# K and V tiles loaded as two halves of 64 partitions from two queues, and w_down in 14 tiles of 128 rows: a decode kernel of two attention and two gated layers

## The chip, the cores and the metric

One core of a Trainium2 chip runs the whole program. The metric is device time in microseconds (us) of one execution. For a program on one core, a run counts as "slow" when it lies over 1.5% above the fastest run of the same kernel, and slow runs are left out of ratios. A ratio below is the mean time of one kernel's fast runs over the mean of the other's fast runs of the same rounds, so it isn't quite the ratio of the medians that are quoted. A kernel is called faster or slower only when its whole interval lies beyond 2%.

In the profile lines PE is TensorE (matmuls), PEld its weight loads, DVE VectorE, ACT ScalarE, POOL GpSimd and SP SyncE. A partition is one of the 128 rows of SBUF, the on-chip memory into which tiles are loaded. A load is cut into packets, which 16 DMA engines move; "DMA share" is the time of all packets over the time of the 16 engines, so 1 means that all are busy. The granted clock (PEclk) is TensorE's clock as a share of full speed.

## The reference, cut to what matters

```python
# B=4 batches, one query row each, D=512; 32 query heads, 8 K/V heads, 4096 positions, head size 128, F=1792; bf16
def A(x, k_cache, v_cache, wq, wo):        # attention over the cache
    q = (x @ wq).reshape(B, 1, 32, 128)...
    p = softmax(q @ k.T * 128**-0.5)       # each K/V head serves 4 query heads
    return (p @ v)... @ wo
def Bm(x, w_gate, w_up, w_down):           # gated block
    return (sigmoid(x @ w_gate) * (x @ w_up)) @ w_down

x = x + A(layernorm(x), k_cache, v_cache, wq, wo)
x = x + Bm(layernorm(x), w_gate, w_up, w_down)
x = x + A(layernorm(x), k_cache, v_cache, wq, wo)     # the same caches and weights again
x = x + Bm(layernorm(x), w_gate, w_up, w_down)
```

K and V of one head and one batch are 1 MB each. Both layers read all of them: 2 x 8 x 4 x 2 tiles of 1 MB, 134 MB of the 148 MB that the kernel loads. The rest are weights, which are loaded once, in the first layer.

## The kernel before

A "group" is one K/V head of one layer (16 groups); each needs four K tiles and four V tiles (one for each batch). All tiles go through a ring of ten buffers, all by SyncE's queue, and a load waits until the tile that had its buffer has been used. Each K tile is transposed in place by VectorE before TensorE multiplies.

```python
    ring = [sb(f"ring{i}", [P, T * DH], bf) for i in range(NS)]     # P=128, T*DH=4096, NS=10
    wd = sb("wd", [FR, 4, 4, D], bf)                                # FR=112: 1792 = 112 * 16
    ...
    def load_kv(n, kind, b):
        s = len(tiles) % NS
        ...
        if kind == "k":      # each partition: one run of 8 KB
            i = A_k[b, g].rearrange("(p t) d -> p (t d)", p=P)
            o = dst[:]
        else:                # each partition: four runs of 2 KB
            i = A_v[b, g].rearrange("(a p t) d -> p a (t d)", a=4, p=P)
            o = dst[:].rearrange("p (a x) -> p a x", a=4)
        S.put("sp", lambda e: e.dma_start(o, i), writes=[f"r{s}"], dma=f"r{s}")
    ...
        (7, "k"): [lambda: load_w(          # w_down goes out after the K tiles of group 7
            "wd", wd[:].rearrange("r j c n -> r j (c n)"), B_wd.rearrange("(j r c) n -> r j (c n)", j=4, c=4)
        )],
```

The only other work of GpSimd is building constants at the start and one small operation (`rstd`) in each of the four norms.

## Time and profile before

| | before |
|---|---|
| time, median of 2 runs | 415.18 us (414.91 to 415.44) |
| bytes read | 148.1 MB, all K, V and weights on one queue |
| rate in layer 2, where nothing but K and V is loaded (260 to 370 us) | 403 GB/s |
| VectorE waiting for K loads, in total (view of waits) | 53 us |
| TensorE waiting for V loads, in total (view of waits) | 12 us |

These are lines of the page of before: the share of time in which the 16 DMA engines were busy (tenths, 40 slices of the span), the rate in each slice; then two groups of instructions (busy us, mean ns of one, then idle time just before them and what ended most of it); then the DMA issues (KB each, median us from issue to landing).

```profile
DMA  7999999999999999999999919999999999999500
GB/s 260 408 382 413 386 389 406 391 415 386 406 391 394 403 407 415 396 416 281 293 411 396 359 25 392 407 401 405 401 407 399 407 399 407 400 407 399 209 2 0
...
L333 DVE STREAM_TRANSPOSE ring<-ring 128x2048 int32<-128x2048 int32 x64 | 146.2, 2299 | 53.7 <-DMA ring<-in_A_k_cache_dram 53.3
...
L413 PE MATMUL O_ps<-ring,pt_sb 128*16 128x512 bf16 x512 | 57.3, 628 | 27.4 <-ACT pt_sb L374 15.9
...
ring<-in_A_k_cache_dram SPq DMA_DIRECT2D x64, 1024.0 KB, 14.2
ring<-in_A_v_cache_dram SPq DMA_DIRECT2D x64, 1024.0 KB, 16.2
...
wd<-in_B_w_down_dram SPq DMA_DIRECT2D x1, 1792.0 KB, 30.9
```

The DMA engines are busy in nearly every slice, at about 400 GB/s, and the computing engines wait for them: the loads bound the kernel. Four places fall short: the first slice; slices 19 and 20 (281 and 293 GB/s); slice 24 (25 GB/s), where all ten buffers are full and the chain of matmuls and norms between the layers has to finish; and the end. The load of w_down takes twice as long to land (30.9 us) as the typical load of K or V (14 to 16 us).

The view of stretches gives the same in numbers. Its columns are: from and to, length, busy us and instructions of each computing engine, granted clock of TensorE, share of DMA time, GB/s.

```profile
core 0: us, PE busy (x) PEld busy (x) DVE busy (x) ACT busy (x) POOL busy (x), PEclk, DMA share, GB/s
187.00:208.00 21.00, 5.93 (x39) 1.64 (x38) 10.30 (x6) 2.41 (x2) 0.00 (x0) 0.50 1.03 288
239.00:249.50 10.50, 5.00 (x72) 2.34 (x72) 3.08 (x7) 1.65 (x6) 0.54 (x1) 0.67 0.14 24
260.00:370.00 110.00, 61.58 (x570) 25.13 (x568) 63.72 (x74) 26.91 (x56) 0.00 (x0) 0.60 1.03 403
```

The DMA view of 186 to 210 us alone, in 40 slices of 0.6 us, shows what happens around the load of w_down:

```profile
DMA  9999999999998999999999999999999999999999
GB/s 410 410 423 437 437 396 410 253 218 253 205 171 191 225 266 253 212 218 218 215 242 198 215 218 201 229 239 239 277 369 375 369 386 376 379 389 393 382 399 382
```

While the packets of w_down are in flight, the rate stays between 171 and 277 GB/s, about 225 in the mean and little over half of the normal one, although the engines are fully busy.

The trace also keeps each DMA packet with its size and time. Worked out from that record (medians):

```
before   K packets     8192 B   313 ns      (8192)
before   V packets     2048 B    88 ns      (34816, with those of wq)
before   w_down        4096 B   294 ns      (448)
```

The 66 K packets that start while those of w_down do (189.8 to 205.5 us) take 547 ns in the mean and 566 in the median.

### The profile page before, as it was taken

What the parts mean: (1) busy time and instruction counts of PE and PEld (TensorE: products, weight loads), DVE (VectorE), ACT (ScalarE), POOL (GpSimd) and SP (SyncE); (2) the same over time, 40 slices, a digit from 0 to 9 for tenths busy, and PEclk for the clock granted to TensorE, in tenths of its full rate; (3) what the DMA queues carried; (4) which work ended last, traced back from release to release, by engine and by line L of the source; (5) the groups of instructions that cost most, each with busy time, mean ns of one, the idle gap of its engine ahead of it and who ended that gap; (6) DMA issues with size and microseconds to landing.
All of it is one profiled execution on the core that took longest, in us unless ns stands there. A gap on an engine that the chain in (4) does not pass through costs nothing.

```text
span 415.9 us, 4348 instructions
## 1 busy us (share of the span) xinstructions
PE 203.4 (49%) x1784; PEld 84.8 (20%) x1784; DVE 205.9 (50%) x259; ACT 82.5 (20%) x179; POOL 6.7 (2%) x24
## 2 busy tenths in 40 slices
PE   0047343473545447352316745475745555654556
PEld 0013111121212212120002222131312222221122
DVE  3823627346272825516316626473829283838221
ACT  1031040210403031040210014132231303030300
POOL 4000000000000000000000000000000000000000
PEclk9985565555555555555555766655556666566659
DMA  7999999999999999999999919999999999999500
GB/s 260 408 382 413 386 389 406 391 415 386 406 391 394 403 407 415 396 416 281 293 411 396 359 25 392 407 401 405 401 407 399 407 399 407 400 407 399 209 2 0
DMA packets 50067, 148.40 MB, mean 357 GB/s; under 512 B 2232, under 2 KB 6336, under 8 KB 41600
## 3 DMA queue, kind: packets, MB, share of 16 engines
q1 hardware_dynamic: 50048, 148.13, 93.6%
q8 instruction: 14, 0.23, 0.2%
q14 instruction: 5, 0.04, 0.0%
HBM read 148.12 MB, written 0.00 MB: 356 GB/s over the span
## 4 chain that ended last, share of the span: by engine, by line
issue 40%; DMA 28%; PE 14%; DVE 7%; SPq 6%; ACT 4%; POOL 0%; POOLq 0%; ACTq 0%; DVEq 0%
DMA ring<-in_A_k_cache_dram 24%; PE S_ps L342 5%; SPq L222 5%; DMA ring<-in_A_v_cache_dram 5%; DVE ring L333 3%; PE O_ps L413 3%; ACT p_sb L358 2%; PE Y_ps L499 2%; PE M_ps L429 1%; DVE ml L352 1%; SPq L235 1%; PE Y_ps L446 1%; PE PT_ps L471 1%; PE O_ps L471 1%; ACT o_sb L424 1%
## 5 line engine op out<-in xcount | busy, mean ns | idle before, releaser
L333 DVE STREAM_TRANSPOSE ring<-ring 128x2048 int32<-128x2048 int32 x64 | 146.2, 2299 | 53.7 <-DMA ring<-in_A_k_cache_dram 53.3
L342 PE MATMUL S_ps<-ring,qbd 128*16 128x512 bf16 x512 | 57.0, 620 | 82.4 <-DVE ring L333 81.4
L358 ACT ACTIVATE p_sb<-S_ps,nbias 128x1024 bf16<-128x1024 f32 x16 | 40.4, 2522 | 185.8 <-DVE nbias L355 185.8
L413 PE MATMUL O_ps<-ring,pt_sb 128*16 128x512 bf16 x512 | 57.3, 628 | 27.4 <-ACT pt_sb L374 15.9
L352 DVE TENSOR_REDUCE ml<-S_ps 128x1 f32<-128x1024 f32 x16 | 19.6, 1224 | 60.9 <-PE S_ps L342 60.9
L342 PEld LDWEIGHTS S_ps<-ring,qbd 128*16 128x16 bf16 x512 | 15.4, 120 | 121.2 <-DVE ring L333 81.5
L429 PE MATMUL M_ps<-sel_o,o_sb 128*128 128x16 f32 x128 | 26.9, 349 | 14.0 <-ACT o_sb L424 14.0
L429 PEld LDWEIGHTS M_ps<-sel_o,o_sb 128*128 128x128 f32 x128 | 25.3, 294 | 28.5 <-ACT o_sb L424 28.5
L317 PE MATMUL Q_ps<-qT,perm 128*128 128x16 bf16 x64 | 4.4, 179 | 51.5 <-ACT qT L314 51.5
L446 PE MATMUL Y_ps<-wo,oT 128*4 128x512 bf16 x64 | 26.5, 560 | 4.7 <-ACT oT L435 4.7
L413 PEld LDWEIGHTS O_ps<-ring,pt_sb 128*16 128x16 bf16 x512 | 15.8, 125 | 56.9 <-issue 38.8
L379 DVE STREAM_TRANSPOSE tr<-ml 128x64 f32<-128x64 f32 x16 | 3.9, 245 | 42.2 <-ACT qT L314 37.0
L424 ACT ACTIVATE o_sb<-O_ps,wcol 128x512 f32<-128x512 f32 x16 | 11.0, 687 | 68.3 <-PE O_ps L413 64.6
L323 ACT ACTIVATE qbd<-Q_ps 32x64 bf16<-32x64 f32 x64 | 13.7, 214 | 6.6 <-PE Q_ps L317 6.0
L317 PEld LDWEIGHTS Q_ps<-qT,perm 128*128 128x128 bf16 x64 | 2.9, 107 | 52.8 <-ACT qT L314 52.8
L369 PE MATMUL PT_ps<-sel_p,p_sb 128*128 128x64 bf16 x128 | 9.4, 238 | 8.3 <-ACT p_sb L358 8.3
L393 DVE TENSOR_TENSOR el<-ee,tr 128x16 f32<-128x16 f32 x16 | 2.8, 175 | 20.2 <-ACT ee L392 20.2
L309 PEld LDWEIGHTS Q_ps<-xnT,wq 128*128 128x128 bf16 x256 | 7.9, 102 | 13.3 <-issue 12.9
L309 PE MATMUL Q_ps<-xnT,wq 128*128 128x4 bf16 x256 | 9.2, 166 | 1.6 <-DMA wq<-in_A_wq_dram 1.3
L374 ACT ACTIVATE pt_sb<-PT_ps 128x512 bf16<-128x512 f32 x16 | 9.6, 597 | 1.9 <-PE PT_ps L369 1.5
L456 DVE SCALAR_TENSOR_TENSOR x_row<-Y_ps,x_row 4x512 f32<-4x512 f32 x4 | 2.7, 679 | 14.0 <-PE Y_ps L446 8.8
L293 PE MATMUL M_ps<-sel_h,xn 4*128 4x4 bf16 x16 | 1.2, 173 | 16.9 <-DVE xn L286 16.9
(53 smaller groups left out, 88.7 us busy)
## 6 DMA issues: line engine op xcount, KB each, us to landing
ring<-in_A_k_cache_dram SPq DMA_DIRECT2D x64, 1024.0 KB, 14.2
ring<-in_A_v_cache_dram SPq DMA_DIRECT2D x64, 1024.0 KB, 16.2
wq<-in_A_wq_dram SPq DMA_DIRECT2D x4, 1024.0 KB, 14.9
wo<-in_A_wo_dram SPq DMA_DIRECT2D x4, 1024.0 KB, 14.8
wg<-in_B_w_gate_dram SPq DMA_DIRECT2D x1, 1792.0 KB, 15.7
wu<-in_B_w_up_dram SPq DMA_DIRECT2D x1, 1792.0 KB, 15.7
wd<-in_B_w_down_dram SPq DMA_DIRECT2D x1, 1792.0 KB, 30.9
x_io<-in_A_x_dram SPq DMA_DIRECT2D x1, 4.0 KB
```

The source lines that it names most:

```text
L222: S.put("sp", lambda e: e.dma_start(o, i), writes=[f"r{s}"], dma=f"r{s}")
L309: fns.append(lambda e, h=h, k=k, c0=c0: e.matmul(Q_ps[:, h * B:(h + 1) * B], lhsT=wq[:, k, c0:c0 + DH], rhs=xnT[:, k, :], start=(k == 0), ...
L323: fns.append(lambda e, a=a: e.activation(qbd[32 * a:32 * a + 32, qi, :, :, a * R:(a + 1) * R], Q_ps[32 * a:32 * a + 32, 64:128].rearrange( ...
L333: S.put("dve", lambda e: e.transpose(v, v), reads=[f"r{s}"], writes=[f"r{s}"])
L342: fns.append(lambda e, q=q, nn=nn, b=b, kt=kt: e.matmul(S_ps[32 * b:32 * b + 16, q * 512:(q + 1) * 512], lhsT=qbd[:, qi, b, nn, :], rhs=kt ...
L352: "dve", lambda e: e.tensor_reduce(ml[:, 0:1], S_ps[:], AX.X, ALU.max, negate=True),
L358: lambda e: e.activation(p_sb[:].rearrange("p tb (j q) -> p q tb j", q=4), S_ps[:].rearrange("p (q tb j) -> p q tb j", q=4, tb=8), ACTF.Ex ...
L374: "act", lambda e: e.activation(pt_sb[:].rearrange("p t x -> p (t x)"), PT_ps[:], ACTF.Copy),
L413: fns.append(lambda e, tb=tb, b=b, v=v: e.matmul(O_ps[32 * b:32 * b + 16, :], lhsT=pt_sb[:, tb, 16 * b:16 * b + 16], rhs=v[:, :, tb, :], s ...
L424: "act", lambda e: e.activation(o_sb[:], O_ps[:], ACTF.Copy, scale=wcol[:, 0:1]),
L429: fns.append(lambda e, a=a: e.matmul(M_ps[:, 0:16], lhsT=o_sb[:, a * P:(a + 1) * P], rhs=sel_o[:, a, :], start=(a == 0), stop=(a == 3),))
L446: fns.append(lambda e, h=h: e.matmul(Y_ps[0:B, :], lhsT=oT[:, g * R + h, :], rhs=wo[:, g * R + h, :], start=(g == 0 and h == 0), stop=(g = ...
```

## The change

The intent: more bandwidth from two queues that work at the same time, and an end to the dip at w_down, whose load has 112 partitions. Each K and V tile is cut into partitions 0 to 63, issued by SyncE, and 64 to 127, issued by GpSimd. w_down is laid out as three chunks of 128 rows for each quarter of F (12 tiles) and two tiles that stack the four remainders of 64 rows.

```diff
-    wd = sb("wd", [FR, 4, 4, D], bf)
+    wd = sb("wd", [P, 4, 3, D], bf)
+    wd_r = sb("wd_r", [P, 2, D], bf)
...
-        S.put("sp", lambda e: e.dma_start(o, i), writes=[f"r{s}"], dma=f"r{s}")
+        for q, eng in ((0, "sp"), (1, "pool")):
+            if kind == "k":
+                oo, ii = o[64 * q:64 * q + 64], i[64 * q:64 * q + 64]
+            else:
+                oo, ii = o[64 * q:64 * q + 64], i[64 * q:64 * q + 64]
+            S.put(eng, lambda e, oo=oo, ii=ii: e.dma_start(oo, ii), writes=[f"r{s}{'ab'[q]}"], dma=f"r{s}{'ab'[q]}")
...
+    def load_wd():
+        rows = B_wd.rearrange("(j f) n -> j f n", j=4)
+        load_w("wd", wd[:]..., rows[:, 0:FM, :].rearrange("j (p c) n -> p j (c n)", c=3))     # FM = 384
+        for i in range(2):
+            load_w(f"wd_r{i}", wd_r[i * FR:(i + 1) * FR], rows[2 * i:2 * i + 2, FM:FS, :]...)  # FR = 64
...   (readers of a tile wait for both halves; the down projection has 14 matmuls instead of 16)
```

## The prediction

> **What bounds the kernel now.** The loads do. The page shows 148.1 MB on one queue, 93.6% of the engines' time; the table of stretches gives 400 GB/s from 10.4 to 187 us and 403 GB/s from 260 to 387 us while PE and DVE are half busy. In the raw packet records a K packet (8 KB) takes 313 ns and a V packet (2 KB) 88 ns: about 12 ns fixed and 27 B/ns per engine, so the limit (estimate: 16 x 27.2 = 435 GB/s) is only 8% away. Losses outside that: the start (260 GB/s for 10 us); 187 to 208 us at 288 GB/s; 239 to 249.5 us, where the ten ring buffers are full and the chain waits for GLU, norm and scores (24 GB/s); and a tail of 28 us after the last loads.
>
> **w_down.** The loss at 187 to 208 us is the load of w_down: 448 packets of 4 KB took 294 ns instead of about 163 (estimate from 12 ns + 27 B/ns), the load landed after 30.9 us, and its neighbours were slowed too (K packets to about 546 ns, V to 119). The DMA view shows a flat 215 GB/s there, half rate. My reading: with 112 partitions engines share SBUF ports. The stretch lost about 21 x (1 - 288/400) = 5.9 us. Loads of 128 partitions plus two small ones of 64 should win back 4 to 6 us. It is on the critical path (values of group 7 wait 8.7 us for V right after). Two matmuls less save under 0.5 us per layer.
>
> **Halves.** Bytes and packet sizes stay; the number of K/V issues doubles. SyncE isn't short of issue time, so a second issuer removes nothing there. What may be gained is the 12 ns between packets, if two rings per engine overlap: at most 7%, mainly V. The risk: each half lies in 64 partitions. The Trainium skill, "SBUF — State Buffer", Door 1, says partitions 0..63 reach eight of 16 ports (196 GB/s measured) and that two concurrent DMAs at partitions 0 and 64 were only 6% faster than one. No run here shows halves, but the 215 GB/s of w_down is the same pattern. With both rings filled, pairs of engines share two ports: taking turns, they keep 400 GB/s; in step, they get about 215. K/V is 134 MB: each 10% of rate lost costs about 35 us.
>
> GpSimd adds about 7 us of constants before its first load (timeline: busy until 7.1 us), during which the lower half runs alone: 1 to 3 us. In layer 1 SyncE's queue also carries 14 MB of weights, so the halves drift apart; a tile is complete only with its slower half.
>
> **Sum.** 415 - 5 (w_down) + 2 (start) = 412 if the halves are neutral; about 395 if overlap pays; 450 to 650 if ports collide. Collision is somewhat likelier than not: predicted 428 us, range 396 to 620. Faster 0.24, same 0.24, slower 0.52.
>
> **What would show it.** Collision: DMA still about 100% busy, GB/s of 260 to 400 in the steady stretches, K packets well over 313 ns, PE and DVE waiting for ring loads. Overlap: 410 to 430 GB/s. w_down: no dip before the layer boundary. Drift: one half's landing time well above the other's.
>
> **What would make it wrong.** Fabric buffering that lets engines take turns by themselves; GpSimd too slow in writing descriptors, so that its half limits; another mapping of 64 partitions to engines.

## The result, and the profile after

The changed kernel takes 622.79 us (621.53 and 624.06), half as much again as before: the ratio is 1.501, with a 95% interval of 1.4918 to 1.5102. The page of the changed kernel, the same lines:

```profile
DMA  8999999999999999999999989999999999999920
GB/s 199 240 270 260 245 233 279 250 241 290 238 228 257 231 256 226 262 273 239 256 238 258 229 193 239 274 240 262 261 245 255 273 250 269 253 265 263 260 43 0
...
q1 hardware_dynamic: 29920, 81.02, 55.9%
q0 software_dynamic: 14336, 67.12, 41.5%
...
L350 DVE STREAM_TRANSPOSE ring<-ring 128x2048 int32<-128x2048 int32 x64 | 147.0, 2306 | 249.7 <-DMA ring<-in_A_k_cache_dram 248.9
L430 PE MATMUL O_ps<-ring,pt_sb 128*16 128x512 bf16 x512 | 56.4, 619 | 161.7 <-DMA ring<-in_A_v_cache_dram 135.2
...
ring<-in_A_k_cache_dram SPq DMA_DIRECT2D x64, 512.0 KB, 26.2
ring<-in_A_v_cache_dram SPq DMA_DIRECT2D x64, 512.0 KB, 29.6
ring<-in_A_k_cache_dram POOLq DMA_DIRECT2D x64, 512.0 KB, 14.9
ring<-in_A_v_cache_dram POOLq DMA_DIRECT2D x64, 512.0 KB, 16.3
```

The DMA engines are as busy as before, to the end, but they move about 250 GB/s instead of 400. The idle time before the K transposes grows from 53.7 to 249.7 us, that of TensorE before the values from 27.4 to 161.7 us; most of both now ends with a load. GpSimd's halves land 15 to 16 us after their issue, SyncE's only after 26 to 30 us.

Two stretches of the changed kernel, the start and a piece of layer 2 (without weight loads):

```profile
0.00:10.40 10.40, 0.00 (x0) 0.00 (x0) 3.34 (x9) 1.28 (x1) 8.00 (x26) 1.00 0.76 188
430.00:580.00 150.00, 50.47 (x468) 21.68 (x468) 52.17 (x66) 24.07 (x55) 19.95 (x35) 0.54 1.03 259
```

Layer 2 runs at 259 GB/s. The packet record shows that the packets themselves became slow (medians):

```
after    K packets, SyncE     8192 B   529 ns      (4096)      before: 313 ns
after    K packets, GpSimd    8192 B   522 ns      (4096)
after    V packets, SyncE     2048 B   142 ns      (18432, with those of wq)   before: 88 ns
after    V packets, GpSimd    4096 B   231 ns      (8192)
```

GpSimd's V packets are twice as large as SyncE's: the same transfer is cut differently by the two queues.

### The profile page after: what moved, and what is told of

Same layout as the page of the kernel before. It is cut to its first block, busy times and chain, and to the rows that moved or that the text cites. A ratio compares the mean times of both kernels' runs of the same rounds, so it can differ in the third digit from the quotient of the medians.

```text
span 622.2 us, 4600 instructions
## 1 busy us (share of the span) xinstructions
PE 200.0 (32%) x1782; PEld 82.7 (13%) x1782; DVE 207.0 (33%) x259; ACT 82.5 (13%) x179; POOL 79.9 (13%) x152
## 4 chain that ended last, share of the span: by engine, by line
DMA 62%; SPq 13%; PE 11%; issue 8%; DVE 3%; ACT 1%; POOL 0%; POOLq 0%; ACTq 0%; DVEq 0%
DMA ring<-in_A_v_cache_dram 48%; DMA ring<-in_A_k_cache_dram 14%; SPq L229 9%; PE O_ps L430 7%; SPq L242 4%; PE Y_ps L521 2%; PE S_ps L359 1%; DVE ring L350 1%; ACT p_sb L375 1%; PE PT_ps L488 1%; PE O_ps L488 0%; DVE ml L369 0%; ACT qbd L340 0%; DVE x_row L473 0%; DVE xn L303 0%
## 5 line engine op out<-in xcount | busy, mean ns | idle before, releaser
L350 DVE STREAM_TRANSPOSE ring<-ring 128x2048 int32<-128x2048 int32 x64 | 147.0, 2306 | 249.7 <-DMA ring<-in_A_k_cache_dram 248.9
L430 PE MATMUL O_ps<-ring,pt_sb 128*16 128x512 bf16 x512 | 56.4, 619 | 161.7 <-DMA ring<-in_A_v_cache_dram 135.2
L229 POOL DMA_DIRECT2D ring<-in_A_v_cache_dram x64 | 40.0, 634 | 249.5 <-PE O_ps L430 229.4
L229 POOL DMA_DIRECT2D ring<-in_A_k_cache_dram x64 | 33.6, 530 | 232.3 <-PE Q_ps L326 203.9
L446 PE MATMUL M_ps<-sel_o,o_sb 128*128 128x16 f32 x128 | 23.7, 321 | 13.9 <-ACT o_sb L441 13.9
L446 PEld LDWEIGHTS M_ps<-sel_o,o_sb 128*128 128x128 f32 x128 | 22.0, 260 | 27.6 <-ACT o_sb L441 27.6
L463 PE MATMUL Y_ps<-wo,oT 128*4 128x512 bf16 x64 | 23.6, 508 | 4.7 <-ACT oT L452 4.7
L521 PE MATMUL Y_ps<-wd,hT 128*4 128x512 bf16 x24 | 10.0, 601 | 0.6 <-DVE hT L515 0.6
```

The costliest lines, as they stand in the source:

```text
L229: S.put(eng, lambda e, oo=oo, ii=ii: e.dma_start(oo, ii), writes=[f"r{s}{'ab'[q]}"], dma=f"r{s}{'ab'[q]}")
L350: S.put("dve", lambda e: e.transpose(v, v), reads=[f"r{s}a", f"r{s}b"], writes=[f"r{s}a", f"r{s}b"])
L430: fns.append(lambda e, tb=tb, b=b, v=v: e.matmul(O_ps[32 * b:32 * b + 16, :], lhsT=pt_sb[:, tb, 16 * b:16 * b + 16], rhs=v[:, :, tb, :], s ...
L446: fns.append(lambda e, a=a: e.matmul(M_ps[:, 0:16], lhsT=o_sb[:, a * P:(a + 1) * P], rhs=sel_o[:, a, :], start=(a == 0), stop=(a == 3),))
L463: fns.append(lambda e, h=h: e.matmul(Y_ps[0:B, :], lhsT=oT[:, g * R + h, :], rhs=wo[:, g * R + h, :], start=(g == 0 and h == 0), stop=(g = ...
L521: fns.append(lambda e, i=i, l=l, r=r: e.matmul(Y_ps[0:B, :], lhsT=l, rhs=r, start=(i == 0), stop=(i == len(parts) - 1),))
```

## The experiments

My theory was the *port theory*. The Trainium skill, "DMA: Bandwidth & Descriptors", section "The descriptor swizzle", says that a transfer of 128 partitions is dealt to the 16 engines so that each engine writes one SBUF port. A half of 64 partitions reaches only eight ports ("SBUF — State Buffer", Door 1); if it still goes over 16 engines, two engines have to share a port. (The prediction puts the 6% for two concurrent DMAs under Door 1 as well; on that page it stands in a section of its own, named in the last section here.) Rivals: *GpSimd* (writing descriptors is slow), *two queues* (engines that alternate between queues lose time), *smaller transfers* (512 KB instead of 1 MB), and *the memory that is read*.

Twelve kernels ran. Unless said otherwise each is the changed kernel with the edit shown, and all have the new w_down. The record doesn't say which of the 16 engines moved a packet, so the port theory can be tested by its consequences alone. In four of the kernels (e5, e9, e10, e11) the result is wrong on purpose. The comparison with the reference passed for these too, so its tolerance doesn't see the attention part.

### e1: the w_down part alone

```diff
-        for q, eng in ((0, "sp"), (1, "pool")): ...
+        S.put("sp", lambda e: e.dma_start(o, i), writes=[f"r{s}a"], dma=f"r{s}a")     # whole tile
```

> The w_down part of the change alone: K and V tiles are whole again (128 partitions, SyncE's queue), w_down is loaded as one piece of 128 partitions and two of 64. If my reading of the dip at 187 to 208 us is right (a load of 112 partitions makes engines share SBUF ports), the dip goes and the time is 409 to 411 us, 4 to 6 us under before. If the dip had another cause (the place in the program, the memory behind w_down), the time stays within 1 us of 415. It says at the same time how much of the 208 us of loss the w_down part could carry: none.

Measured: 408.27 us (407.83 to 408.60, 4 runs) against 415.99 of before in the same rounds, ratio 0.9813 (0.9772 to 0.9854). Stretches of this run:

```profile
187.00:208.00 21.00, 4.90 (x43) 1.42 (x40) 11.72 (x14) 3.22 (x4) 0.00 (x0) 0.50 1.04 367
235.00:242.00 7.00, 3.87 (x48) 1.44 (x48) 1.38 (x2) 2.00 (x3) 0.00 (x0) 0.74 0.30 97
260.00:370.00 110.00, 60.72 (x572) 25.31 (x572) 64.94 (x80) 29.79 (x66) 0.00 (x0) 0.61 1.03 404
```

The stretch of 187 to 208 us moves 367 instead of 288 GB/s, with w_down's packets of 3 KB at 126 ns. The w_down part is a gain of 1.9%, a little more than I expected (the interval reaches past 2%, so at the 2% line the verdict is "unclear"), and all of the loss is due to the halves. What is left of the dip belongs to the two pieces of 64 partitions: from 190 to 194 us, with w_down's 128-partition piece in flight, the rate is 399 GB/s, from 194 to 198 us, with their 1 KB packets among the others, 262, and V's packets take 132 ns in the median. The gain shows further on: the timeline has the values of group 7 start at 211.3 instead of 217.6 us, and the nearly empty stretch between the layers shrinks from about 10.5 to 7 us. A part of that isn't the change: in 210 to 230 us this run was granted a TensorE clock of 0.72, before 0.50. (Between runs the clock explains little: before's seven runs of these rounds were granted 0.61 to 0.66 and took 414 to 417 us in no order of clock.)

### e2, e3, e4: one queue, another cut, another issuer

e2 keeps the cut and issues both halves from SyncE; e3 keeps the two queues and cuts along the free dimension, so that each half has 128 partitions; e4 keeps the cut and replaces GpSimd by ACT, another hardware queue.

```diff
# e2
-        for q, eng in ((0, "sp"), (1, "pool")):
+        for q, eng in ((0, "sp"), (1, "sp")):
# e3
-                oo, ii = o[64 * q:64 * q + 64], i[64 * q:64 * q + 64]            # k
+                oo, ii = o[:, 2048 * q:2048 * q + 2048], i[:, 2048 * q:2048 * q + 2048]
-                oo, ii = o[64 * q:64 * q + 64], i[64 * q:64 * q + 64]            # v
+                oo, ii = o[:, 2 * q:2 * q + 2], i[:, 2 * q:2 * q + 2]
# e4
-        for q, eng in ((0, "sp"), (1, "pool")):
+        for q, eng in ((0, "sp"), (1, "act")):
```

> The changed kernel with one edit: both halves of 64 partitions go out from SyncE's queue. Port theory (a half reaches eight ports, and two engines then share one): on one queue the halves come one after the other, so nearly all of the time only one set of eight ports is written; 205 to 250 GB/s, 620 to 690 us, no better than the changed kernel. GpSimd theory (descriptors written by GpSimd, or its queue, slow the loads): back to 405 to 420 us. Two-queue theory (engines that alternate between two queues lose time): also back to 405 to 420 us.

> The changed kernel with one edit: the halves are cut along the free dimension (each has all 128 partitions, 4 KB of a K row or two of the four V pieces), still one from SyncE and one from GpSimd, still 512 KB each. Port theory: every engine writes its own port again, 400 GB/s or more, 400 to 415 us. GpSimd, two-queue and small-transfer (512 KB) theories: it stays slow, 550 to 630 us.

> The changed kernel with one edit: the upper half of 64 partitions is issued by ACT instead of GpSimd, so it goes by another hardware queue and GpSimd writes no descriptors. Port theory: as slow as the changed kernel, 590 to 660 us, K packets of 8 KB still over 480 ns. GpSimd theory: 405 to 420 us. Two-queue theory: slow as well, so this run alone doesn't tell it from ports; the halves along the free dimension do.

Measured: e2 651.58 us in its fast run and 669.95 in a run counted as slow; e3 424.48 us (423.33 to 426.22, ratio 1.021, 1.0165 to 1.0255); e4 590.32 us (587.55 and 593.10, ratio 1.419). The stretches of layer 2, first e2 (its profile is of the slow run, so take it as a rough value), then e3, then e4:

```profile
430.00:620.00 190.00, 60.03 (x554) 25.43 (x551) 61.19 (x71) 25.62 (x56) 0.00 (x0) 0.55 1.04 227
```

```profile
260.00:370.00 110.00, 62.07 (x540) 26.01 (x532) 65.19 (x74) 25.83 (x57) 27.36 (x44) 0.55 1.03 398
```

```profile
430.00:550.00 120.00, 50.56 (x426) 22.66 (x427) 51.35 (x58) 20.88 (x46) 0.00 (x0) 0.56 1.03 291
```

Turning the cut by 90 degrees takes the rate in layer 2 from 259 back to 398 GB/s, with two queues, GpSimd and 512 KB all kept. That rules out these three as the main cause, by one edit. The edit also halves K's packets to 4 KB, but V's packet sizes stay, and these recover too: SyncE's 2 KB packets from 142 to 88 ns, GpSimd's 4 KB packets from 231 to 167 ns. Taking the second queue or GpSimd away, and keeping the cut, doesn't bring the rate back: one queue gives 227 GB/s, ACT in GpSimd's place 291 (and 5% less time). e3 took 9 us more than I allowed for; see e6 to e8.

### e5: one half alone

```diff
-        for q, eng in ((0, "sp"), (1, "pool")):
+        for q, eng in ((0, "sp"),):          # upper halves: set to zero once, never loaded
```

> Measures the limit of one set of ports by itself; the result is wrong on purpose. Only the lower half of each K and V tile (partitions 0 to 63) is loaded, from SyncE's queue; the upper halves stay zero and nothing goes through GpSimd. K and V are then 67 MB. Port theory: the second layer, which has no weight loads, runs at 205 to 220 GB/s, K packets of 8 KB take about 600 ns, and the whole takes 370 to 400 us. If 64 partitions alone were not the limit (only the mix of two halves or two queues), these loads run near 400 GB/s until compute binds, K packets stay near 313 ns, and the whole takes 230 to 290 us.

Measured: 421.56 us (a second run, 436.78, was slow). The total is a miss (370 to 400 us were expected). The zeroing of ten upper halves keeps VectorE busy until 24.7 us, but that isn't the reason: the DMA share is 1.01 and 1.07 from 10.4 to 20 and 20 to 30 us, so no load time was lost there. The 81 MB take about 380 us at the rates seen; what the expectation left out is rather the stall between the layers (52 and 77 GB/s from 240 to 260 us) and the 24 us after the last load packet. The rate is what the run was for; layer 2:

```profile
280.00:390.00 110.00, 64.87 (x568) 27.20 (x572) 68.40 (x79) 27.01 (x62) 0.00 (x0) 0.56 1.04 204
```

204 GB/s, and the packets take about twice their time: 8 KB 636 ns (313 before), 2 KB 169 ns (88). The DMA share is 1.04, so it isn't that half of the engines stood idle. So 64 partitions by themselves are limited to half of the rate, on one queue and with nothing else in flight. A doubling is what two engines at one port would give; the trace doesn't say which engine moved which packet, so the pairing itself is argued. The Trainium skill ("SBUF — State Buffer", Door 1) has 196 GB/s for 64 partitions and about 218 as the limit of eight ports; this run agrees.

### e11: the memory or the ports?

Halves along the free dimension from SyncE (e8, below), but each K half reads the same 512 KB of memory as in the changed kernel, spread over 128 partitions.

```diff
+                half = A_k[b, g][2048 * q:2048 * q + 2048, :]
+                oo, ii = o[:, 2048 * q:2048 * q + 2048], half.rearrange("(p t) d -> p (t d)", p=P)
```

> Tells the memory that is read from the SBUF partitions that are written. Base is the run with halves along the free dimension, both from SyncE (415 us). Each K half now reads the very same 512 KB of memory as a half of the changed kernel (rows 0 to 2047 or 2048 to 4095), but spreads it over all 128 partitions (4 KB each; wrong order on purpose). Port theory: only the written partitions matter, so 410 to 418 us and 4 KB packets at 160 to 170 ns. If reading half of a tile's memory at a time were the slow thing: K packets of 4 KB near 265 ns and well over 500 us.

Measured: 414.51 us (413.65 and 415.37), K packets of 4 KB at 161 ns. Layer 2:

```profile
260.00:370.00 110.00, 60.19 (x580) 24.95 (x580) 61.24 (x75) 28.44 (x63) 0.00 (x0) 0.59 1.04 398
```

For K, the memory that is read doesn't matter (V's halves were not tested in this way). The partitions that are written do.

### e9 and e10: why 259 GB/s, and neither 215 nor 400

Both start from e4 (both halves on hardware queues, packets of one kind cut alike). e9 loads K with V's pattern, in pieces of 2 KB; e10 loads V with K's pattern, in pieces of 8 KB.

```diff
# e9, in the branch for k
-            i = A_k[b, g].rearrange("(p t) d -> p (t d)", p=P)
-            o = dst[:]
+            i = A_k[b, g].rearrange("(a p t) d -> p a (t d)", a=4, p=P)
+            o = dst[:].rearrange("p (a x) -> p a x", a=4)
# e10: the opposite edit in the branch for v
```

> Why two halves in flight together reach 250 GB/s and neither 215 nor 400. Base is the run with the halves from SyncE and ACT (590 us), where K packets of 8 KB took 530 ns (313 when alone) but V packets of 2 KB only 104 to 107 ns (88). Here K is loaded with V's pattern (four pieces of 2 KB in each partition; the scores are wrong on purpose). Packet theory: an engine alternates between the two queues packet by packet, short packets to the two sets of ports interleave, long ones block each other; then K's 2 KB packets take 100 to 120 ns and the time falls to 530 to 560 us. If size doesn't matter (K is slow for another reason, such as where it is in the order), they take about 145 ns and the time stays at 575 to 610 us.

> The opposite edit on the same base (SyncE and ACT, 590 us): V is loaded with K's pattern, one piece of 8 KB in each partition (wrong result on purpose). Packet theory: V's packets then take about 530 ns as K's do, and the time rises to 610 to 650 us, although long packets save the fixed 12 ns. If size doesn't matter: 570 to 600 us.

Measured: e9 520.79 us in its fast run (530.06 in one counted as slow), e10 642.47 us (640.88 and 644.06, ratio 1.5427), with e4 at 590 between them. Layer 2 of e9, then of e10:

```profile
330.00:480.00 150.00, 70.76 (x676) 32.29 (x672) 73.94 (x95) 34.01 (x75) 0.00 (x0) 0.63 1.04 340
```

```profile
430.00:600.00 170.00, 64.10 (x532) 27.89 (x532) 63.03 (x71) 25.17 (x56) 0.00 (x0) 0.54 1.02 253
```

Packets of 2 KB, median: 98 ns in e9, 11% over the 88 ns of before (in the mean 109 against 90, 21% over). Packets of 8 KB: 525 and 527 ns in e10, 68% over. So two halves in flight on two queues lose little with short packets and much with long ones. It isn't that one queue ran dry: in both runs the two queues have 40 to 60% of the DMA time each in 69 slices of 2 us (of 75 and 85), and these slices alone move 352 (e9) and 254 GB/s (e10). That engines take turns at a port in one case and block each other in the other is the reading that fits; why it depends on the size no run shows. It may also be why the changed kernel is slower than e4: GpSimd cuts V into packets of 4 KB, and these took 231 ns, while two of e4's 2 KB packets took about 210; and SyncE's 2 KB packets beside them took 142 instead of 107 ns, which is the larger part. The drift of the halves (below) is a second possible reason; no run parts the two.

### e6, e7, e8 and e12: what the second queue costs when the ports are clean

e3 has clean ports and still takes 16 us more than e1. e8 is e3 with both halves from SyncE; e6 sends whole tiles, those of batches 1 and 3 from GpSimd; e7 sends all whole tiles from GpSimd; e12 is e6 with half of the weights moved to GpSimd.

```diff
# e6 (in place of the loop over halves)
+        eng = ("sp", "pool")[b % 2]
+        S.put(eng, lambda e: e.dma_start(o, i), writes=[f"r{s}a"], dma=f"r{s}a")
# e7:  eng = "pool"          e8: e3's cut, for q, eng in ((0, "sp"), (1, "sp"))
# e12: e6, and in load_w
+        eng = "pool" if key in ("wq1", "wo0", "wo1", "wo3", "wg", "wd_r1") else "sp"
```

> Halves along the free dimension as in the run at 424 us, but both from SyncE's queue. If the 16 us over w_down alone came from the second queue or from GpSimd, this returns to 406 to 412 us; if they came from the smaller transfers (512 KB) and smaller K packets (4 KB instead of 8 KB), it stays at 418 to 428 us. From packet times alone I expect a part of it: 4 KB packets took 164 ns against 156 for half of an 8 KB one, 5% of the K time, 8 us.

> Whole tiles of 128 partitions and 1 MB, those of batches 0 and 2 from SyncE, of 1 and 3 from GpSimd, with the new w_down. Two queues and GpSimd's descriptors stay, the ports are clean. It tells what cost the 16 us between the halves along the free dimension (424 us) and w_down alone (408 us): if it was the size of 512 KB, this is back at 406 to 411 us; if it was two queues with the weights on one of them, or GpSimd, it stays at 418 to 430 us.

> Whole tiles of 128 partitions, all from GpSimd, weights from SyncE, with the new w_down. If writing descriptors on GpSimd limits anything, this doubles it: over 430 us. If GpSimd's queue is as good as SyncE's, 405 to 420 us, the upper end if weights that share the engines with K and V arrive too early or too late.

> Whole tiles alternating between SyncE and GpSimd as in the run at 422 us, with one edit: about half of the weight loads (wq1, wo0, wo1, wo3, w_gate, a piece of w_down) go out from GpSimd. Drift theory: there the weights delayed SyncE's tiles while GpSimd's ran ahead, the last values of layer 1 started 7 us later than with one queue and the stall at the boundary lasted 15 us instead of 7; balanced queues should bring 408 to 414 us. If two queues cost by themselves, it stays at 419 to 424 us.

| run | edit against e1 | us, median | ratio to before (95%) |
|---|---|---|---|
| e1 | none | 408.27 | 0.9813 (0.9772 to 0.9854) |
| e7 | all tiles from GpSimd | 410.30 | 0.9848 (0.9801 to 0.9894) |
| e8 | halves along the free dimension, one queue | 414.74 | 0.9948 (0.9915 to 0.9981) |
| e12 | whole tiles alternate, weights on both queues | 421.25 | 1.0111 (1.0079 to 1.0144) |
| e6 | whole tiles alternate, weights on SyncE's | 422.46 | 1.0136 (1.0100 to 1.0172) |
| e3 | halves along the free dimension, two queues | 424.48 | 1.0210 (1.0165 to 1.0255) |

GpSimd as the issuer costs nothing that can be told (e7 against e1). Smaller transfers cost about 6 us (e8 against e1): the times of all K packets, summed and divided by 16 engines, are 168 us at 4 KB and 162 us at 8 KB. Two queues at once cost 10 to 14 us (e6 against e1, e3 against e8), and not in the steady state. Stretches of layer 2 in e8, then of e6, the stall between the layers and layer 2:

```profile
260.00:370.00 110.00, 59.28 (x580) 24.82 (x576) 62.05 (x78) 29.06 (x64) 0.00 (x0) 0.61 1.04 398
```

```profile
234.00:249.00 15.00, 8.78 (x91) 3.67 (x91) 6.33 (x11) 1.10 (x6) 1.83 (x3) 0.77 0.03 7
260.00:370.00 110.00, 63.16 (x565) 26.00 (x563) 62.51 (x73) 24.96 (x55) 13.04 (x20) 0.55 1.03 403
```

Layer 2 runs at 403 GB/s as before, but the stall lasts about 15 us (7 in e1), because the values of group 7 start at 218.1 instead of 211.3 us; and in the last group the scores start at 387.6 us and the values at 396.5 (e1: 375.5 and 384.3), 9 us apart in both, close to the end of the loads. (Some 2.6 us more of this pair of runs lie after the start of the last values, 25.1 us against 22.5, where e6 was granted a clock of 0.60 and e1 0.83 from 385 us on.) GpSimd's tiles land 12 to 13 us after issue, SyncE's 17 to 19: later tiles of one queue overtake those that are needed next on the other. I thought that the weights on SyncE's queue were the reason. e12 says no: with weights on both, its landing times stay as far apart (12 to 14 against 18 to 20 us), and so does the stall:

```profile
236.00:251.00 15.00, 8.70 (x85) 3.38 (x83) 5.20 (x9) 1.70 (x6) 1.89 (x3) 0.82 0.08 12
```

That theory fell. The packet record has one reason that I overlooked. In 78 slices of 1 us of e6 both queues move V and hardly anything else: GpSimd's queue moves 241 GB/s there and SyncE's 145, with 4586 and 5471 packets. GpSimd's packets are 4 KB and SyncE's 2 KB, so about equal numbers of packets make unequal shares (e12: 237 and 148 GB/s in 94 slices). Where both move K, in 8 KB packets on either queue, the shares are 197 and 223 GB/s (43 slices). No run with equal V packets on both queues and whole tiles (ACT in GpSimd's place) tested whether this removes the cost. How much of the 10 to 14 us comes from the order of landing stays open.

e1 is the best of all kernels that ran: 1.9% faster than before, and its interval (0.9772 to 0.9854) lies wholly below 1, though not wholly beyond 2%.

## Why the prediction was wrong, point by point

- **Loads bound the kernel, before and after: right.** The DMA share stays full in both, and the computing engines wait longer for loads.
- **w_down, 4 to 6 us: right in kind, a little small.** Done alone it gave 7.7 us (difference of medians). The layout of 112 partitions was the reason for the dip: while the piece of 128 partitions is in flight there is none (399 GB/s). Its packets are 3 KB instead of 4, but that isn't it: e8's 4 KB packets to 128 partitions took 161 ns, w_down's 294. That engines shared ports there is argued.
- **GpSimd's constants delay the start by 1 to 3 us: right in kind.** The first 10.4 us moved 188 instead of 260 GB/s, 0.75 MB less, which is 2 us at 400 GB/s and 3 us at the rate of the changed kernel. The late start of GpSimd costs this only together with the cut: e6, with the same constants and whole tiles, moved 258 GB/s in these 10.4 us.
- **Packet sizes stay: wrong.** GpSimd cut V into 4 KB packets where SyncE has 2 KB.
- **Gain from overlapping packets of two queues, up to 7%: not seen.** With clean ports, two queues gave 398 (e3) and 403 GB/s (e6) in layer 2, one queue with tiles of the same cut 398 (e8) and 404 (e1).
- **Halves drift apart: they do (15 against 26 to 30 us to landing), but that is a small part of the cost.** Of 75 slices of 2 us in layer 2 (430 to 580 us), SyncE's queue has over 85% of the DMA time in 9, at 213 GB/s; in the 10 in which each has 40 to 60% the rate is 261, hardly better than the 259 of the whole.
- **The step that failed is the term "Halves" in the sum.** The text named the right mechanism and its price ("in step, they get about 215", "450 to 650 if ports collide") and then weighed it against "taking turns, they keep 400 GB/s", so that the central figure was 428 us and the range ended at 620. That left a term of 16 us over the neutral sum of 412 us where the chip showed about 211 (622.8 - 412). The chance for slower, 0.52, was too low for the same reason. What stood against taking turns was in the trace already: around w_down K's packets of 8 KB took 547 ns in the mean instead of 318. In the changed kernel they take 548 (SyncE) and 526 (GpSimd).
- **What the runs put in its place.** As parts of before's time: w_down -1.9% (e1); smaller transfers about +1.4% (e8 over e1); the second queue about +2.6% (e3 over e8); the cut at partition 64 about +48% (the changed kernel over e3). The cut alone caps a half at 204 GB/s (e5). Two halves in flight reach 259, between the two outcomes that the prediction named, and how much depends on packet size (340 with 2 KB, 253 with 8 KB).

The steps are differences of ratios from runs on more than one chip, each against its own runs of before; I take them as good to about half a per cent.

## What to carry to other kernels

Look at which partitions each single transfer writes, not only at how much is in flight: here a full DMA row in the profile with half of the usual GB/s and packets that take twice as long went with loads that write only half of the partitions (e5), and a second queue with the other half didn't repair it. If a load has to be split, split it along the free dimension and keep 128 partitions in each piece, as e3 and e8 did at 398 GB/s. When a forecast has two outcomes far apart, don't let the range end at the edge of the bad one, and use the worst slowdown that the trace already shows for the same packets.

## What the Trainium skill lacked or had wrong

- "SBUF — State Buffer", section "Can I just issue two DMAs to hit both halves?": two concurrent DMAs, at partitions 0 and 64, are given as 6% faster than one. Here two halves on two queues reached 259 GB/s against 204 for one alone (27% more), and 340 GB/s (67% more) with packets of 2 KB on both queues. The page has no word on packet size, on which this depended.
- "DMA: Bandwidth & Descriptors", "Rules for kernel authors": it calls splitting into partition halves something not to bother with, as the two only serialize. The runs show more than that: the time rose by 50%, since one half alone runs at 204 instead of 403 GB/s.
- The same page picks the number of engines by divisibility, so 112 partitions use 16. The full DMA share during that load agrees. The page doesn't say that such a load is slow: here the rate fell to about 225 GB/s while it was in flight, its 4 KB packets took 294 ns, and it slowed the loads beside it (8 KB packets to 547 ns in the mean).
- "DMA: Bandwidth & Descriptors", "Issuing engines are not separate DMA queues": issuing from several engines is said to save issue time and nothing more. With clean ports it cost 10 to 14 us here (e6 against e1, e3 against e8). The two queues' shares were unequal for V (241 and 145 GB/s in e6); how much of the cost that explains, these runs don't show.
- No page says that the same V transfer is cut into 2 KB packets from SyncE and 4 KB packets from GpSimd, as the packet record shows.
